# Idle TensorE products, an earlier read of the slot maxima, and a later place for one pair's logits in the last softmax of an attention and slot-MoE kernel

## The chip, the cores and the metric

The kernel runs on one core of a Trainium2 chip. The metric is the device time of one execution in microseconds (us). PE is the matrix engine, DVE the vector engine, ACT the activation engine, POOL the general engine that also issues the loads, SP the engine that issues the stores.

## The reference

The input is q, k and v of 8 batches, 12 heads, 448 tokens and 64 values a head, and the weights phi (768 x 32), w1 (8 experts, 768 x 1024) and w2 (8 experts, 1024 x 768), all float32. The output has 3584 rows of 768.

```python
scores = scale * q @ k^T ;  m = max(scores, -1)
e = exp(scores - m)
attn = e / (sum(e) + exp(-m) + 1e-9)
x = (attn @ v) as rows of 768            # 3584 x 768, heads side by side
logits = x @ phi                         # 3584 x 32 slots
d = softmax of logits over the 3584 rows # for each slot
slot_input = d.T @ x                     # 32 x 768, four slots for each expert
slot_out[e] = relu(slot_input[e] @ w1[e]) @ w2[e]
c = softmax of logits over the 32 slots  # for each row
out = c @ slot_out
```

The softmax `d` runs over all rows, so no expert can start before the last batch's logits are known. This is where the change lies.

## The kernel before

The order of work is written out by hand; each engine carries out its own list in order, and waits are added where one engine reads what another wrote. Two engines that read the same PSUM tile are ordered as well.

Attention goes by pairs of heads: 48 pairs, six to a batch, numbered 0 to 47. The main loop takes a step `s` for each pair, with two halves, numbered `hs = 2*s + y`. In a half step `Bk` makes scores and exponentials, `AV` multiplies the exponentials with v (`AV(n, i, range(3))` for three of four groups of query rows, `AV(n, i, [3])` for the last group), `N1` and `N2` normalize a pair's rows, and `PX` transposes them with four products and copies the result (`xT`) to bf16, on ACT at line 450 (for the last pair half on ACT at line 447 and half on DVE at line 448). In `N2` of the last pair DVE makes the factors and scales three quarters of the rows (lines 407 to 414), and ACT scales the last quarter twice (line 420).

`P(b)` makes the softmaxes of a batch as a list of functions, which the dictionary `post` puts into half steps. The last batch's list is `last`:

- `l_mm([j])` multiplies pair j's transposed rows with phi in both orientations: four products into `ps_lT` (line 486, slots on partitions) and four into `ps_l` (line 477, rows on partitions). Both are parts of one PSUM tile. For pair 0 of the batch the order is reversed.
- `l_ev` copies `ps_l` to SBUF on ACT (line 493). `l_turn` takes the maxima of `ps_lT` on DVE (line 507).
- `s_max` spreads the maxima to all partitions with one product (line 517), reduces them and joins them with the running maximum. `d_sub` subtracts, `exps` takes exponentials on ACT (line 529), `corr` rescales the running sums.
- `s_mm` adds the batch's slot inputs: 28 products (line 544). `s_last` adds them to the running sums and makes the experts' input on DVE (lines 561 to 568).
- `keep_busy(n)` issues n products of 128 x 256 whose result nobody reads (`ps_idle`, line 435).

Pair j of the last batch is pair 42 + j, so "pair 47" is its sixth and last. `last[0]` to `last[3]` (the logits of its first four pairs) are in `post`; `last[3]` falls into half step 96. There it stands between the two parts of pair 47's products with v: `AV(47, 2..3, range(3))`, then `post`, then `AV(47, i, [3])`, `PX(46)`, `N1(47)`, `N2(47)`. Behind the loop POOL gets two weight loads (`load_rows`) and two small operations on `own4`, DVE some small operations on constants (lines 718 to 724), and then follow:

```python
keep_busy(1)
last[4]()
PX(NPAIR - 1)
keep_busy(1)
last[5]()
load_rows(35, 37)
load_rows(37, 40)
```

Then the experts, in two groups of four experts side by side. `hidden` makes the w1 products (line 741: 72 in a row for group 0 and half of group 1, later 24), ACT applies relu (line 743), `turn` transposes (lines 748, 749), and `slots` makes the w2 products (line 755), of 384 columns, four experts abreast. `slots(0, range(4))` comes first (32 products), then a transpose, then 96 in a row: `slots(0, range(4, 8))`, and for each half of the output columns `slots(1, range(8), [half])`, row by row of the weights with the four experts of group 1 inside. The w2 weights of experts 3 to 7 are loaded late, row by row (40 rows of 128 x 768), into SBUF that attention frees: `load_rows(37, 40)` brings expert 7's rows 5 to 7 over the batch's x tile, which `s_mm` reads. All weight loads are issued by POOL (line 112).

The output stage multiplies with `c` (line 811), scales on ACT and DVE (lines 817, 819) and stores from SP (line 822) in seven transfers.

Of the kernel before, what the change touches and what calls it, by code (L numbers as in the profile page):

```python
# [31 lines left out]
def kernel(  # L32
# [10 lines left out]
    nc = tc.nc  # L43
    B, H, S, D = q.shape
    DD = H * D
    NS = moe_phi.shape[1]
# [3 lines left out]
    KC = DD // 128  # L50
    FK = F // 128
    ND = DD // 2
    PB = H // 2
    NPAIR = B * PB
# [18 lines left out]
    phi_sb = const.tile([128, KC, NS], BF16, name="phi_sb")  # L73
# [26 lines left out]
    xT = lambda b, j: part("xTa", j * 512, 512) if b < B - 1 and j < 4 else part("xTb", (j % 2) * 512, 512)  # L100
# [32 lines left out]
    with ExitStack() as at:  # L133
# [296 lines left out]
        def keep_busy(n):  # L430

            if "idle" not in st:
                st["idle"] = pb_("ps_idle")
            for _ in range(n):
                nc.tensor.matmul(st["idle"][:, 0:256], ident, w_sb["w1", 0][:, 0, 0:256], start=True, stop=True)

        def PX(n):
            b, pb = divmod(n, PB)
            x, c = xb[b % 2], slice(pb * 128, pb * 128 + 128)
            two = n == NPAIR - 1  # L440
            pss = [pb_("ps_x") for _ in range(1 + two)]
            for i in range(4):
                o = (i % 2 if two else i) * 128
                nc.tensor.matmul(pss[i // 2 if two else 0][:, o:o + 128], x[:, i, c], ident if i < 3 else ident2,  # L444
                                 start=True, stop=True)
            if two:
                nc.scalar.copy(xT(b, pb)[:, 0:256], pss[0][:, 0:256])
                nc.vector.tensor_copy(xT(b, pb)[:, 256:512], pss[1][:, 0:256])
            else:
                nc.scalar.copy(xT(b, pb), pss[0])  # L450
# [7 lines left out]
        def P(b):  # L458
# [3 lines left out]
            v = {}  # L462
# [3 lines left out]
            def l_mm(js):  # L466
                if js[0] == 0:
                    if b < B - 1:
                        v["ps_l"] = pa([128, 4, NS], F32, "ps_l")
                    else:  # L470
                        t = psV.tile([128, 512], F32, tag="v", name="ps_l")
                        v["ps_l"] = t[:, 0:4 * NS].rearrange("p (i s) -> p i s", i=4)
                        v["ps_lT"] = t[:, 4 * NS:4 * NS + 128]

                def plain(j):
                    for i in range(4):
                        nc.tensor.matmul(v["ps_l"][:, i, :], xT(b, j)[:, i * 128:(i + 1) * 128], phi_sb[:, j, :],
                                         start=(j == 0 and i == 0), stop=(j == KC - 1), skip_group_check=True)

                for j in js:  # L480
                    if b < B - 1 or j == 0:
                        plain(j)
                    if b == B - 1:

                        for i in range(4):
                            nc.tensor.matmul(v["ps_lT"][NS * i:NS * i + NS, :], phi_sb[:, j, :],
                                             xT(b, j)[:, i * 128:(i + 1) * 128],
                                             start=False, stop=(j == KC - 1), skip_group_check=True)
                        if j:
                            plain(j)  # L490

            def l_ev():
# [33 lines left out]
            def exps(z0=0, z1=8):  # L526
                if "cd" not in v:
                    v["cd"] = psm.tile([128, 8, NS], BF16, tag="cd", name="cd", bufs=1)
                nc.scalar.activation(flat(v["cd"][:, z0:z1, :]), flat(v["z"][:, z0:z1, :]), AF.Exp)
# [40 lines left out]
            both = lambda *fs: (lambda: [f() for f in fs])  # L570
            if b < B - 1:
                return [both(lambda: l_mm(range(KC)), l_ev, c_max), both(l_turn, c_sub), both(s_max, d_sub),
                        both(exps, corr)] + ([c_turn, both(s_mm, s_add)] if late(b) else [both(s_mm, s_add), c_turn])
            return [lambda: l_mm([0]), lambda: l_mm([1]), lambda: l_mm([2]), lambda: l_mm([3]), lambda: l_mm([4]),
                    both(lambda: l_mm([PB - 1]), l_ev, l_turn, lambda: keep_busy(1), s_max,
                         d_sub, lambda: exps(4, 8), corr, lambda: keep_busy(4), s_mm, s_last, lambda: keep_busy(2),
                         c_max, c_sub, lambda: exps(0, 4)),
                    c_turn]

# [2 lines left out]
        post = {}  # L582
        for b in range(B - 1):
            for z, f in enumerate(P(b)):
                at_z = (0, 1, 2, 4, 6, 9) if late(b) else (0, 1, 2, 3, 4, 6)
                post.setdefault(2 * (PB * b + PB + 2) + at_z[z], []).append(f)
# [9 lines left out]
        hrec = psm.tile([128, 1], F32, name="hrec", bufs=1)  # L596
        cscale = take(F + (KC + 10) * NS, 8 * B).bitcast(F32).rearrange("p (h b i) -> p h b i", h=2, i=4)
        last = P(B - 1)
        for z in range(4):
            post.setdefault(2 * NPAIR - 5 + 2 * z - (z == 3), []).append(last[z])  # L600


        runs = [(n, i) for n in range(NPAIR) for i in range(4)]
# [118 lines left out]
        nc.gpsimd.affine_select(out=own4, in_=own4, fill=1.0, compare_op=ALU.not_equal, base=0,  # L722
                                pattern=[[-16, 2], [-36, 4], [-1, 4]], channel_multiplier=1)
        nc.vector.reduce_max(own, own4, axis=AX.X)
        keep_busy(1)
        last[4]()
        PX(NPAIR - 1)
        keep_busy(1)
        last[5]()
        load_rows(35, 37)  # L730
        load_rows(37, 40)
# [46 lines left out]
        for half in range(2):  # L778
            for bp in range(B // 2):
                o = (half * (B // 2) + bp) * 4  # L780
                nc.tensor.matmul(ps_cs[:, o:o + 4], cT[:, bp, half, :, :].rearrange("p b j -> p (b j)"), band,
                                 start=True, stop=True)
# [70 lines left out]
```

## Time and profile before

| | us |
|---|---|
| median of 3 runs | 311.84 (311.04 to 312.73) |
| profiled execution, its own time | 313.42 |
| its span, first to last instruction | 311.6 |
| PE busy | 279.1 (90%) |
| DVE busy | 250.9 (81%) |
| ACT busy | 247.4 (79%) |
| POOL busy | 196.9 (63%) |
| mean granted TensorE clock | 0.944 |

The profile is one execution. A timeline row gives the start and length in us from the span's start, engine, line, operation, output and input tile, count, and in brackets the idle time before it with what ended it. A row of the windows gives, for a stretch of time, each engine's busy time and count, then the granted PE clock (1 is full speed), the mean busy share of the 16 DMA engines and GB/s. PE rows end where the model of the pipeline has the last result, which is later than the point at which the next product starts.

### The profile page before, as it was taken

The numbers are of one execution on the slowest core, as the hardware profiler recorded it, in microseconds if no ns is written. First come the engines' busy times: TensorE is split into PE (matmuls) and PEld (weight loads), VectorE is DVE, ScalarE is ACT, GpSimd is POOL, SyncE is SP. The second block draws the span as 40 slices with busy tenths as digits, with TensorE's granted clock in tenths as the row PEclk, the third lists the DMA queues.
The fourth block names the chain that finished last, engine by engine and source line by source line (L and its number), as shares of the span: only waits on it lengthen the run. The fifth ranks groups of instructions, "written<-read, shape, count | busy, mean of one in ns | idle before, by whom it ended". The sixth has DMA issues, their size and how long they took to land.

```text
span 311.6 us, 12145 instructions
## 1 busy us (share of the span) xinstructions
PE 279.1 (90%) x5070; PEld 160.7 (52%) x5070; DVE 250.9 (81%) x575; ACT 247.4 (79%) x546; POOL 196.9 (63%) x402
## 2 busy tenths in 40 slices
PE   2899899999999999999999999999999996997800
PEld 1444466565566566656556665566655554461100
DVE  4777999999989999998999899989997455237910
ACT  2357499999999999999899999998999984218700
POOL 8642778879878987697979688976776713000000
PEclk9999999999999999999999999999999998697555
DMA  6990399999999999687999999999445999935997
GB/s 86 150 130 12 45 203 207 198 190 169 190 196 166 208 172 208 78 129 126 207 156 187 171 203 154 194 181 160 79 53 103 161 191 210 211 72 214 449 439 312
DMA packets 36934, 54.30 MB, mean 174 GB/s; under 512 B 2576, under 2 KB 27664, under 8 KB 36496
## 3 DMA queue, kind: packets, MB, share of 16 engines
q0 software_dynamic: 35872, 42.52, 84.8%
q1 hardware_dynamic: 1008, 11.01, 8.3%
q8 instruction: 39, 0.64, 0.8%
q14 instruction: 15, 0.12, 0.1%
HBM read 85.03 MB, written 11.01 MB: 308 GB/s over the span
## 4 chain that ended last, share of the span: by engine, by line
PE 68%; DVE 15%; ACT 6%; issue 3%; POOL 3%; POOLq 0%
PE ps_av L386 14%; PE ps_a L240 10%; PE ps_t L216 7%; PE ps_b L320 6%; DVE mx L242 6%; PE ps_b L323 6%; PE ps_b L349 5%; DVE mx L253 3%; PE ps_b L352 3%; PE ps_o L811 3%; PE ps_x L444 3%; PE ps_h L741 2%; PE ps_a L249 2%; PE ps_s L544 2%; ACT W L817 2%
## 5 line engine op out<-in xcount | busy, mean ns | idle before, releaser
L242 DVE TENSOR_REDUCE mx<-ps_a 128x1 f32<-128x448 f32 x246 | 135.3, 612 | 3.3 <-PE ps_a L240 2.6
L325 ACT ACTIVATE W<-ps_b 128x448 bf16<-128x448 f32 x246 | 118.4, 575 | 0.2 <-PE ps_a L240 0.2
L240 PE MATMUL ps_a<-W 64*128 64x448 bf16 x246 | 79.9, 352 | 0.0
L320 PE MATMUL ps_b<-W 64*128 64x448 bf16 x246 | 67.8, 352 | 0.3
L323 PE MATMUL ps_b<-mT,sel 64*128 64x448 bf16 x246 | 65.5, 350 | 0.0
L386 PE MATMUL ps_av<-W 128*128 128x65 bf16 (+1 forms) x1536 | 65.2, 196 | 0.3 <-issue 0.3
L386 PEld LDWEIGHTS <-W 128*128 128x128 bf16 (+1 forms) x1536 | 50.4, 101 | 27.6 <-issue 23.6
L414 POOL TENSOR_TENSOR W<-ubuf,rec 128x384 bf16<-128x384 f32 x44 | 36.2, 823 | 37.8 <-DVE rec L408 24.3
L355 ACT ACTIVATE W<-ps_b 128x448 bf16<-128x448 f32 x90 | 47.5, 568 | 8.0 <-PE ps_b L352 8.0
L216 PEld LDWEIGHTS <-W 64*64 64x64 bf16 x1344 | 31.2, 113 | 19.2 <-issue 8.0
L216 PE MATMUL ps_t<-ident,W 64*64 64x64 bf16 x1344 | 32.1, 198 | 5.8 <-DMA W<-in_q_dram 4.2
L112 POOL DMA_DIRECT2D W<-in_moe_w_dram x37 | 24.7, 669 | 13.7 <-PE ps_s L544 5.1
L450 ACT CAST W<-ps_x 128x512 bf16<-128x512 f32 x47 | 28.1, 599 | 5.9 <-PE ps_x L444 5.7
L262 DVE TENSOR_REDUCE mx<-ps_a 128x1 f32<-128x448 f32 x48 | 29.4, 613 | 0.6 <-PE ps_a L259 0.3
L349 PE MATMUL ps_b<-W 64*64 64x448 bf16 (+1 forms) x138 | 28.9, 380 | 0.1
L240 PEld LDWEIGHTS <-W 64*128 64x128 bf16 x246 | 23.0, 94 | 9.8
L219 ACT COPY W<-ps_t 128x896 bf16<-128x896 bf16 x20 | 18.8, 940 | 11.3 <-PE ps_t L216 11.1
L253 DVE TENSOR_REDUCE mx<-ps_a 128x1 f32<-128x448 f32 x42 | 23.7, 617 | 4.5 <-PE ps_a L249 4.2
L352 PE MATMUL ps_b<-mT,sel 64*64 64x448 bf16 (+1 forms) x138 | 27.0, 362 | 0.0
L323 PEld LDWEIGHTS <-sel 64*128 64x128 bf16 x246 | 20.0, 94 | 12.4 <-issue 2.2
L398 ACT COPY ubuf<-ps_av 128x455 f32<-128x455 f32 x44 | 25.2, 574 | 1.2 <-PE ps_av L386 1.0
L423 POOL TENSOR_TENSOR W<-ubuf,rec 128x128 bf16<-128x128 f32 x44 | 17.5, 398 | 3.7
(133 smaller groups left out, 440.1 us busy)
## 6 DMA issues: line engine op xcount, KB each, us to landing
W<-in_moe_w_dram POOLq DMA_DIRECT2D x25, 768.0 KB, 9.8
out_dram<-W SPq DMA_DIRECT2D x3, 2688.0 KB, 11.1
W<-in_v_dram POOLq DMA_DIRECT2D x32, 192.0 KB, 6.2
W<-in_q_dram POOLq DMA_DIRECT2D x15, 336.0 KB, 6.6
W<-in_k_dram POOLq DMA_DIRECT2D x15, 336.0 KB, 7.4
W<-in_moe_w_dram POOLq DMA_DIRECT2D x5, 576.0 KB, 10.1
out_dram<-W SPq DMA_DIRECT2D x3, 768.0 KB, 4.2
W<-in_moe_w_dram POOLq DMA_DIRECT2D x1, 960.0 KB, 9.7
```

What stands on the lines that cost most here:

```text
L216: nc.tensor.transpose(ps[r, a, c:c + 64], src[r, pl, tok * D:(tok + 1) * D], ident[r, r])
L240: nc.tensor.matmul(ps[:, 0:S], t[r, 0, i * 128:(i + 1) * 128], t[r, 1, :], start=True, stop=True)
L242: nc.vector.reduce_max(m[:, c:c + 1], ps[:, 0:S], axis=AX.X)
L253: nc.vector.reduce_max(mx[g][:, c:c + 1], pss[hl][:, 0:S], axis=AX.X)
L320: nc.tensor.matmul(pss[hl][:, 0:S], t[rs[hl], 1, cols], t[rs[hl], 0, :], start=True, stop=False)
L323: nc.tensor.matmul(pss[hl][:, 0:S], sel[rs[hl], 2 * pl + hl:2 * pl + hl + 1].to_broadcast([64, 128]), mT[mg(n)][rs[hl], :], start=False, s ...
L325: nc.scalar.activation(e[:, hl, :], pss[hl][:, 0:S], AF.Exp, scale=scale)
L349: nc.tensor.matmul(outs[hl], t[rs[hl], 1, cols], t[rs[hl], 0, :], start=True, stop=False)
L352: nc.tensor.matmul(outs[hl], sel[rs[hl], 2 * pl + hl:2 * pl + hl + 1].to_broadcast([64, m]), mT[mg(n)][rs[hl], :], start=False, stop=True)
L355: nc.scalar.activation(e, p[:, 0:S], AF.Exp, scale=scale)
L386: nc.tensor.matmul(o, eT[n, i, hl][:, qc], vp[g % 2][:, 2 * pl + hl, i, 0:W65], start=(i == 0 and u == 0 and hl == 0), stop=(i == 3), skip ...
L414: eng.tensor_mul(x[:, 0:3, c:c + 128].rearrange("p i (h d) -> p i h d", h=2), u[:, 0:6, 0:D].rearrange("p (i h) d -> p i h d", h=2), rec[: ...
```

## The change

1. The fourth pair's logits, `last[3]`, leave half step 96 and are called behind the loop, so they stand behind `AV(47, i, [3])` and `PX(46)` on PE.
2. Idle products: ahead of `last[4]` six in place of one, ahead of `last[5]` two in place of one, behind the last logits two in place of one, behind the spread of the maxima twelve in place of four.
3. `l_turn` comes ahead of `l_ev`: DVE reads the maxima from PSUM first, ACT copies the logits afterwards.
4. The last pair's logits go by halves: two products into `ps_lT` and two into `ps_l` for the first two row tiles, then the same for the other two.

No instruction of DVE, ACT or POOL is added or removed. POOL's and SP's order is the same; on ACT and DVE only the waits of the two readers differ. PE gets 15 more idle products.

```diff
-                def plain(j):
-                    for i in range(4):
+                def plain(j, tiles=range(4)):
+                    for i in tiles:
                         nc.tensor.matmul(v["ps_l"][:, i, :], xT(b, j)[:, i * 128:(i + 1) * 128], phi_sb[:, j, :],
...
-                        for i in range(4):
-                            nc.tensor.matmul(v["ps_lT"][NS * i:NS * i + NS, :], phi_sb[:, j, :],
-                                             xT(b, j)[:, i * 128:(i + 1) * 128],
-                                             start=False, stop=(j == KC - 1), skip_group_check=True)
-                        if j:
+                        for i0 in (0, 2):
+                            for i in (i0, i0 + 1):
+                                nc.tensor.matmul(v["ps_lT"][NS * i:NS * i + NS, :], phi_sb[:, j, :],
+                                                 xT(b, j)[:, i * 128:(i + 1) * 128],
+                                                 start=False, stop=(j == KC - 1), skip_group_check=True)
+                            if j == KC - 1:
+                                plain(j, (i0, i0 + 1))
+                        if 0 < j < KC - 1:
                             plain(j)
...
-                    both(lambda: l_mm([PB - 1]), l_ev, l_turn, lambda: keep_busy(1), s_max,
-                         d_sub, lambda: exps(4, 8), corr, lambda: keep_busy(4), s_mm, s_last, lambda: keep_busy(2),
+                    both(lambda: l_mm([PB - 1]), l_turn, l_ev, lambda: keep_busy(2), s_max,
+                         d_sub, lambda: exps(4, 8), corr, lambda: keep_busy(12), s_mm, s_last, lambda: keep_busy(2),
                          c_max, c_sub, lambda: exps(0, 4)),
...
-        for z in range(4):
-            post.setdefault(2 * NPAIR - 5 + 2 * z - (z == 3), []).append(last[z])
+        for z in range(3):
+            post.setdefault(2 * NPAIR - 5 + 2 * z, []).append(last[z])
...
-        keep_busy(1)
+        last[3]()
+        keep_busy(6)
         last[4]()
         PX(NPAIR - 1)
-        keep_busy(1)
+        keep_busy(2)
         last[5]()
```

## The prediction

> **What bounds the kernel now.** I read the 40 slices of the page first: PE is busy nearly everywhere, so only a stretch where it is not can pay. The clock row falls in two places, near 263 and at the end. I then asked for busy time by windows, and set the windows after finding the clock's steps.
>
> ```profile
> core 0: us, PE busy (x) PEld busy (x) DVE busy (x) ACT busy (x) POOL busy (x), PEclk, DMA share, GB/s
> 263.00:264.00 1.00, 0.80 (x5) 0.61 (x6) 0.58 (x3) 0.00 (x0) 0.56 (x1) 0.61 1.09 212
> 270.00:271.00 1.00, 1.00 (x24) 0.53 (x20) 0.00 (x0) 0.06 (x1) 0.00 (x0) 0.98 1.02 201
> 283.00:284.00 1.00, 0.64 (x4) 0.19 (x4) 1.00 (x2) 1.00 (x3) 0.00 (x0) 0.85 0.00 0
> ...
> 256.39:259.81 3.42, 3.11 (x63) 2.24 (x61) 1.96 (x8) 2.04 (x5) 0.53 (x1) 1.00 1.04 209
> 259.81:263.22 3.41, 1.82 (x24) 1.06 (x24) 2.15 (x8) 1.72 (x5) 1.62 (x5) 1.00 1.13 212
> 263.22:266.63 3.41, 2.93 (x43) 1.73 (x47) 2.02 (x8) 0.43 (x2) 0.93 (x2) 0.50 1.03 212
> 266.63:270.05 3.42, 3.42 (x40) 1.28 (x36) 0.89 (x5) 1.00 (x2) 0.00 (x0) 0.50 1.00 205
> 270.05:273.46 3.41, 3.41 (x65) 1.76 (x61) 0.66 (x2) 1.37 (x2) 0.00 (x0) 1.00 1.09 218
> 280.29:283.70 3.41, 1.53 (x18) 0.60 (x15) 1.81 (x3) 2.25 (x4) 0.00 (x0) 1.00 0.00 0
> ```
>
> A mean clock of 0.61 in the first row puts the step from 1 to 0.5 at 263.22; 0.98 puts the return at 270.04, 0.85 the next drop at 283.70. The steps are 6.82 and 13.66 us apart, two and four times 3.41. On that grid the clock falls after a window in which PE was busy for 1.82 of 3.41 us (53%) and after one with 1.53 (45%); 3.11 (91%) kept it, and 2.93 (86%, at half clock) did not bring it back. So the last softmax's chain costs twice: by its own length, and by 6.8 us of half clock.
>
> Next the timeline, which carries the chain.
>
> ```profile
> 257.92 0.53 PE L386 MATMUL ps_av<-W 128*128 128x65 bf16 x12
> 258.12 0.58 ACT L450 CAST W<-ps_x 128x512 bf16<-128x512 f32 x1
> 258.75 0.24 PE L486 MATMUL ps_l<-W,phi_sb 128*32 128x128 bf16 x4 [0.31 <-ACT W L450]
> 259.12 0.32 PE L386 MATMUL ps_av<-W 128*64 128x65 bf16 x8
> 259.38 0.40 PE L444 MATMUL ps_x<-ident,W 128*128 128x128 bf16 x4
> 259.49 0.17 DVE L407 SCALAR_TENSOR_TENSOR rec<-ps_av,ec 128x7 f32<-128x7 f32 x1 [1.29 <-PE ps_av L386]
> 259.61 0.27 PE L435 MATMUL ps_idle<-W,ident 128*128 128x256 bf16 x1
> 259.87 0.58 ACT L450 CAST W<-ps_x 128x512 bf16<-128x512 f32 x1 [1.16 <-PE ps_x L444]
> 259.95 1.06 POOL L112 DMA_DIRECT2D W<-in_moe_w_dram  x2 [2.30 <-PE ps_x L444]
> 260.50 0.24 PE L486 MATMUL ps_l<-W,phi_sb 128*32 128x128 bf16 x4 [0.62 <-ACT W L450]
> 260.65 0.52 ACT L420 ACTIVATE W<-ps_av,rec 128x64 bf16<-128x64 f32 x2 [0.20 <-DVE W L414]
> 260.79 0.67 PE L444 MATMUL ps_x<-ident,W 128*128 128x128 bf16 x4
> 261.52 0.19 DVE L724 TENSOR_REDUCE ubuf<-ubuf 128x2 f32<-128x32 bf16 x1 [0.29 <-POOL ubuf L722]
> 261.62 0.41 DVE L448 CAST W<-ps_x 128x256 bf16<-128x256 f32 x1
> 262.09 0.23 PE L486 MATMUL ps_l<-W,phi_sb 128*32 128x128 bf16 x2 [0.28 <-DVE W L448]
> 262.25 0.27 PE L477 MATMUL ps_l<-phi_sb,W 128*128 128x32 bf16 x4
> 262.56 0.27 ACT L493 COPY lb<-ps_l 128x128 f32<-128x128 f32 x1 [1.03 <-PE ps_l L477]
> 262.85 0.29 DVE L507 TENSOR_REDUCE sm<-ps_l 128x1 bf16<-128x128 f32 x1 [0.82 <-ACT lb L493]
> 263.20 0.29 PE L517 MATMUL ps_bc<-ident,sm 128*128 128x128 bf16 x1 [0.57 <-DVE sm L507]
> 264.80 0.80 PE L544 MATMUL ps_s<-cd,W 128*128 128x32 bf16 x24 [0.46 <-ACT cd L529]
> 266.16 5.97 PE L741 MATMUL ps_h<-W,ubuf 128*32 128x512 bf16 x72
> 276.28 4.08 PE L755 MATMUL ps_so<-W 128*32 128x384 bf16 x96
> ...
> 283.54 13.79 SPq L822 DMA_DIRECT2D out_dram<-W  x7
> ```
>
> The reader is to see a string of one-engine hand-overs from 259.12 to 266.16 with PE mostly waiting, then PE alone to 280.4, then the output, whose queue stays full:
>
> ```profile
> 285.00:310.50 25.50, 9.52 (x41) 1.63 (x40) 11.21 (x12) 9.41 (x11) 0.00 (x0) 0.50 0.99 420
> ```
>
> With a DMA share of 0.99 behind the first output transfer, the end moves one for one with that transfer's start.
>
> **The change part by part.** *Fourth pair's logits behind pair 47's products.* The eight products of 258.75 stood, with a wait of 0.31 us, ahead of the last eight products of pair 47 (259.12), which release its normalization (259.49). Now those eight follow the twelve of 257.92 directly. A row's modelled end lies some 0.16 us behind the next product's start (the pair transposes end at 259.78, the next product starts at 259.61), so they start near 258.45 - 0.16 = 258.29: a gain of 0.83 us; from the full modelled end it would be 0.67. DVE is free by then and everything behind moves by 0.83: normalization 258.66, pair 46's transposes 258.55, their copy on ACT 259.04 to 259.62 (ACT ended the earlier copy at 258.70), the two scalings on ACT to 260.34. POOL's two weight issues (259.95) wait for the same products and move as much; they matter, because L724 on DVE waits for POOL's work behind them and stands ahead of the copy L448. If they didn't move, this gain would be lost: 0 is the lower bound, 0.83 my value, since the last products that read the rows they overwrite are among the moved ones. The moved logits start behind pair 46's transposes at 258.78 and take 0.29 to 0.37 (260.50 to 260.79, 258.75 to 259.12): to 259.07 to 259.15.
>
> *Six idle products.* Nine idle products are in the trace:
>
> ```profile
> L435 PE MATMUL ps_idle<-W,ident x9: 269/417/421, 259.6 to 265.7; 128*128 128x256 bf16 x9
> 263.29 1.06 PE L435 MATMUL ps_idle<-W,ident 128*128 128x256 bf16 x4
> ```
>
> Four at half clock took 1.06, one 0.42: (1.06 - 0.42) / 3 = 0.213 apart, so 0.107 at full clock. Six take 0.64, to 259.71 to 259.79, while the fifth pair's logits wait for ACT until 259.67: at most 0.12 late. That is hidden: their next step, the last pair's transposes, needs its fourth tile from ACT at 260.34 and PE reaches it at 260.2. At half clock the six would take 1.28 and cost 0.4.
>
> *Two idle products before and two after the last pair's logits* (one each before) end inside the waits for ACT and DVE copies: nothing, with about 0.1 us of cover each.
>
> *Logits by halves.* The second half waits for L448 (now 260.79 to 261.20), then has two plain products behind it, not four: the four take 0.27 against some 0.18 for one, so 0.03 each, a gain of 0.05.
>
> *Maxima ahead of the copy.* L507 waited for ACT's copy (262.56 to 262.83). Both read one PSUM tile and the program orders them; now the reduce waits for PE and the copy for the reduce. Gain 262.85 - 262.56 = 0.29. The copy's reader, the subtraction, stands behind the broadcast product and two more steps of DVE, so the copy is covered.
>
> Sum so far 0.83 + 0.05 + 0.29 = 1.17: the broadcast product comes at 262.03, ahead of the step, and takes about 0.07 less at full clock: 1.24.
>
> *Twelve idle products for four* lie between it and the slot sums. At full clock 12 x 0.107 = 1.28 from about 262.1 to 263.4; the slot sums wait for ACT until 264.80 - 1.24 = 263.56. Covered by 0.15. At half clock they take 2.56 and end 1.1 us late.
>
> *The clock.* On this execution's grid the window 259.81 to 263.22 now has gaps only from about 261.1 to 261.26 and 261.9 to 262.03, so PE is busy some 3.1 us of 3.41, the 91% that kept the clock. Then the first expert products, from 264.92, run at full clock. Before, they spent 266.16 to 270.05 at half: 3.89 / 2 = 1.94 us saved. Sum 1.24 + 1.94 = 3.18.
>
> The Trainium skill ("TensorE: Matmul & The Clock Gate", Part 1: The HAM clock gate) has a free-running window of 3413 ns, which agrees with the steps above. Its section "HAM oscillation — how this bites in real kernels" words the rule as no idle gap over about 3.4 us. The trace disagrees: the clock fell with no gap above 0.7 us, so by that rule the added products would buy nothing and the sum would be 1.24.
>
> *What is late next.* The second group's slot products need the last weight rows (expert 7, rows 5 to 7 of 8).
>
> ```profile
> 265.88 0.54 POOL L112 DMA_DIRECT2D W<-in_moe_w_dram  x1 [2.26 <-PE ps_s L544]
> ...
> W<-in_moe_w_dram POOLq DMA_DIRECT2D x1, 576.0 KB, 11.1
> ...
> 273.46:276.87 3.41, 3.41 (x80) 2.25 (x76) 0.82 (x4) 0.69 (x1) 0.00 (x0) 1.00 0.55 110
> 276.87:280.29 3.42, 3.42 (x88) 2.07 (x80) 1.04 (x4) 0.00 (x0) 0.00 (x0) 1.00 0.02 5
> ```
>
> Issued at 265.88, they land 11.1 us later: 276.98. At the queue's 205 to 218 KB a us, 576 KB need 2.8 us; the other 8 are queueing behind earlier rows, and the DMA share is 1.00 or more from 256.39 to 273.46. An issue 1.2 us earlier only waits longer: the landing stays. The first product that reads them is the 24th of the second group (row 5 of 8, fourth expert of four); 32 products of the first group stand ahead, so it is number 56 of the 96 of 276.28: (4.08 - 0.33) / 95 = 0.0395 apart, so 278.45. Slack 1.47 us. Of the 3.18, at most that passes, less some 0.1 for the hand-over: 1.35 us. PE then waits 1.8 us at that product.
>
> **The rivals.** (a) *No wall*: the rows land earlier, because they are issued earlier or the stream isn't full in other executions. All of 3.18: 308.7. For it: the run's own times vary by 1.7 us; against it: shares of 1.00 to 1.13 in each window.
>
> (b) *The wait drops the clock* (the slower side). With 3.18 gained PE would stop at about 275.25 until 277.0. The window 273.46 to 276.87 then has 1.8 us of work in 3.41 (53%), the very share after which the clock fell. Then the last 41 slot products run at half clock: 41 x 0.0395 = 1.6 us, and the selection and first output products 0.3 to 0.7 more: -1.35 + 1.6 + 0.3 = +0.55, to +0.95: 312.4 to 312.8. Against it: those slot products run four abreast, so PE is denser than in the chain's window; and the wait must lie almost wholly in one window, which about half of all positions allow. It decides if 53% of dense work drops the clock.
>
> (c) *The clock still falls at 263.22.* The chain is 1.24 shorter, but 264.92 to 270.05 is half speed, so half of that is given back: 0.62, 311.2. If the step comes earlier, the twelve products are slow too and 1.1 us late: near 311.8.
>
> **How the numbers follow.** The profiled execution took 313.42 (span 311.6 and 1.8 around it), 1.58 above the median 311.84. My sum makes it 312.05. Runs whose window lies otherwise lose less to the clock before, and so gain a little less; I carry 1.35 over to the median as it is: 310.5. Chances: forecast 0.50 (310.5, own range 309.9 to 311.1), (a) 0.17, (b) 0.18, (c) 0.15. For 8 in 10 the range takes in (c) and the lower price of (b), and half way to (a): 309.3 to 312.5. Within 0.5% (1.56 us, about what a measurement of this kernel can tell from no change) is 310.28 to 313.40. Faster than that: all of (a), 0.4 of the forecast, a little of (c): 0.39. Slower: the worst of (b), and a chain delayed by late idle products with the clock low throughout: 0.11. Same: 0.50.
>
> **What would show it.** Right: the reduce of the maxima ends by about 262.0 ahead of the logits' copy; clock 1.00 through 263 to 275; the 72 expert products in about 4.0 us; a PE wait of over 1 us inside the slot products ended by a DMA near 277. Wrong: last rows landing well before 277, no wait there (then a); 0.50 behind the wait (b); slot sums starting behind the twelve idle products, not behind ACT (c).

## The result and the profile after

The changed kernel took 310.73 us (median of 20 runs, 309.53 to 312.25), the kernel before 312.52 (20 runs, 310.86 to 313.83). The ratio is 0.9948, 95% interval 0.9932 to 0.9964: 0.5% faster. By the ratio that is 1.6 us, by the medians 1.8, where 1.35 were forecast. The profiled execution took 310.18, with a span of 308.4.

The timeline of the changed kernel, in the stretch shown before. Line numbers are up to four higher than before from line 486 on. The first row is pair 46's copy on DVE (its last one of line 398). It lies ahead of everything that was changed, and I count from it below. In the trace of before it is at 256.07.

```profile
256.07 0.63 DVE L398 COPY ubuf<-ps_av 128x455 f32<-128x455 f32 x1
```

```profile
255.20 0.63 DVE L398 COPY ubuf<-ps_av 128x455 f32<-128x455 f32 x1
...
257.04 0.78 PE L386 MATMUL ps_av<-W 128*128 128x65 bf16 x20
257.87 0.17 DVE L407 SCALAR_TENSOR_TENSOR rec<-ps_av,ec 128x7 f32<-128x7 f32 x1 [0.55 <-PE ps_av L386]
258.24 0.59 ACT L450 CAST W<-ps_x 128x512 bf16<-128x512 f32 x1 [0.41 <-PE ps_x L444]
258.32 1.06 POOL L112 DMA_DIRECT2D W<-in_moe_w_dram  x2 [1.55 <-PE ps_x L444]
258.36 0.81 PE L435 MATMUL ps_idle<-W,ident 128*128 128x256 bf16 x6
259.11 0.24 PE L487 MATMUL ps_l<-W,phi_sb 128*32 128x128 bf16 x4
260.00 0.41 DVE L448 CAST W<-ps_x 128x256 bf16<-128x256 f32 x1
260.91 0.29 DVE L510 TENSOR_REDUCE sm<-ps_l 128x1 bf16<-128x128 f32 x1 [0.49 <-PE ps_l L477]
261.24 0.27 ACT L496 COPY lb<-ps_l 128x128 f32<-128x128 f32 x1 [1.11 <-DVE sm L510]
261.26 0.23 PE L520 MATMUL ps_bc<-ident,sm 128*128 128x128 bf16 x1 [0.16 <-DVE sm L510]
261.33 1.47 PE L435 MATMUL ps_idle<-W,ident 128*128 128x256 bf16 x12
262.87 0.75 PE L547 MATMUL ps_s<-cd,W 128*128 128x32 bf16 x24
264.17 4.07 PE L745 MATMUL ps_h<-W,ubuf 128*32 128x512 bf16 x72 [0.22 <-DVE ubuf L564]
272.39 2.46 PE L759 MATMUL ps_so<-W 128*32 128x384 bf16 x55
275.20 1.95 PE L759 MATMUL ps_so<-W 128*32 128x384 bf16 x41 [0.35 <-DMA W<-in_moe_w_dram]
...
280.31 13.60 SPq L826 DMA_DIRECT2D out_dram<-W  x7
```

The twenty products of pair 47 with v now stand together. The maxima come ahead of ACT's copy. The 72 expert products take 4.07 us, not 5.97. And the 96 slot products are split after the 55th by a wait for a DMA: the 56th reads the last weight rows, the place named in the prediction. The last load's rows of the issues and the windows on this trace's clock grid:

```profile
263.90 0.54 POOL L112 DMA_DIRECT2D W<-in_moe_w_dram  x1 [1.93 <-PE ps_s L547]
...
W<-in_moe_w_dram POOLq DMA_DIRECT2D x1, 576.0 KB, 11.3
...
258.21:261.62 3.41, 3.11 (x42) 2.04 (x39) 2.23 (x9) 1.74 (x5) 1.68 (x5) 1.00 1.03 203
261.62:265.03 3.41, 3.13 (x57) 2.14 (x59) 2.24 (x11) 0.43 (x2) 0.89 (x2) 1.00 1.10 223
275.27:278.69 3.42, 2.56 (x47) 1.39 (x50) 1.11 (x2) 0.96 (x2) 0.00 (x0) 1.00 0.00 0
```

PE is busy for 3.11 and 3.13 us of 3.41 in the softmax's windows and the clock stays at 1.00. The mean granted clock says the same of the other runs: it is 0.955 to 0.958 in the 20 runs of the changed kernel, and 0.943 to 0.953 in the 49 runs of the kernel before that were made beside the experiments. The last rows land at 263.90 + 11.3 = 275.2, when PE goes on. Without the wait the 56th product would start at 272.39 + 55 x 0.0395 = 274.56: the wait is 0.64 us.

Each step counted from pair 46's copy (a row's start less the start of that copy), for all traces:

```
                       broadcast  slot  first   56th slot  wait  last rows  first output  span's
                       product    sums  expert  product          landed     transfer      end
before                   7.13     8.73  10.08    22.4      0      20.9       27.47        55.58
before, again (e9)       7.21     8.81  10.17    21.8      0      21.1       26.88        55.01
changed                  6.06     7.67   8.97    20.00     0.64   20.0       25.11        53.21
idle only (e1)           7.13     8.68   9.97    20.99     0.6    21.0       26.10        54.21
order only (e2)          6.04     7.65   8.94    21.0      0      20.0       26.08        54.19
no late rows (e3)        6.06     7.67   8.97    19.3      0      20.1       24.45        52.57
late rows last (e4)      6.06     7.67   8.97     -        0      20.0       24.46        52.56
late rows last (e12)     6.06     7.67   8.97     -        0      20.2       24.50        52.62
copy first (e5)          6.36     7.90   9.20    20.14     0.5    20.1       25.25        53.36
logits back (e6)         6.78     8.39   9.69    21.37     1.3    21.3       26.48        54.60
loads, no effect (e7)    6.06     7.67   8.97    20.30     0.9    20.3       25.41        53.53
24 idle (e8)             6.06     8.75  10.05    20.4      0      20.3       25.52        55.29
4 idle of 12 (e10)       6.07     7.67   8.97    20.19     0.8    20.1       25.29        53.41
loads delayed (e11)      6.07     7.68   8.97    21.02     1.6    21.0       26.12        54.25
```

The copy itself stands between 254.37 and 257.39 in these traces, where no kernel differs. That spread is as wide as the scatter of the times, which is why a median of 8 to 12 runs says less here than one trace read from a fixed row. Each line is one execution, though: the steps of the chain agree to 0.1 us between kernels that do not differ in them, the landing to 0.3. e5 to e11 ran only once each, for the trace, and took 310.52, 311.77, 310.16, 313.22, 313.84, 309.61 and 313.48 us, in this order; with that scatter these times are not compared.

### The profile page after: what moved, and what is told of

It reads as the page before. It is cut to its first block, busy times and chain, and to the rows that moved or that the text cites. A ratio compares the mean times of both kernels' runs of the same rounds, so it can differ in the third digit from the quotient of the medians.

```text
span 308.4 us, 12176 instructions
## 1 busy us (share of the span) xinstructions
PE 277.2 (90%) x5085; PEld 160.8 (52%) x5085; DVE 250.7 (81%) x575; ACT 247.1 (80%) x546; POOL 197.4 (64%) x402
## 4 chain that ended last, share of the span: by engine, by line
PE 64%; DVE 15%; ACT 6%; DMA 4%; issue 3%; POOL 3%; POOLq 0%; ACTq 0%
PE ps_av L386 14%; PE ps_a L240 10%; PE ps_t L216 7%; DVE mx L242 6%; PE ps_b L320 6%; PE ps_b L323 6%; PE ps_b L349 5%; DMA W<-in_moe_w_dram 4%; DVE mx L253 3%; PE ps_b L352 3%; PE ps_x L444 3%; PE ps_o L815 2%; PE ps_a L249 2%; ACT W L821 2%; PE ps_s L547 2%
## 6 DMA issues: line engine op xcount, KB each, us to landing
out_dram<-W SPq DMA_DIRECT2D x3, 2688.0 KB, 11.3
```

## The experiments

My theory after the result: the order shortens the chain, the idle products hold the clock, and the last weight rows cut off the rest. The first rival was that the rows are no limit and the wait was chance; the second, that the order alone does it.

**e1: idle products alone.**

```diff
 (kernel before)
-keep_busy(1); last[4]()  ...  keep_busy(1); last[5]()
+keep_busy(6); last[4]()  ...  keep_busy(2); last[5]()
-l_ev, l_turn, keep_busy(1), s_max, ..., keep_busy(4), s_mm
+l_ev, l_turn, keep_busy(2), s_max, ..., keep_busy(12), s_mm
```

> The kernel before with only the idle products changed (6, 2, 2 and 12 for 1, 1, 1 and 4); the order of logits, maxima and copy is the old one. Theory (clock and rows: the idle products hold the clock, and the last weight rows cap what that brings): granted clock 1.00 from 262 to 276, the 72 expert products in 4.1 us and not 6.0, the first of them at most 0.1 us earlier, a DMA wait of 0.1 to 0.6 us inside the slot products, and 1.3 to 1.8 us less time. Rival (the order is what counts; the clock's gain is lost elsewhere): 0 to 0.4 us less. Rival (PE is not kept busy enough without the shorter chain): the clock still falls near 263 and the time is within 0.3 us of before.

Measured: 311.58 (12 runs), ratio to before 0.9973 (0.9948 to 0.9997). In the trace:

```profile
259.74 1.06 POOL L112 DMA_DIRECT2D W<-in_moe_w_dram  x2 [2.29 <-PE ps_x L444]
265.84 4.07 PE L741 MATMUL ps_h<-W,ubuf 128*32 128x512 bf16 x72 [0.22 <-DVE ubuf L561]
276.86 1.95 PE L755 MATMUL ps_so<-W 128*32 128x384 bf16 x41 [0.33 <-DMA W<-in_moe_w_dram]
...
263.00:264.00 1.00, 1.00 (x10) 0.91 (x11) 0.66 (x3) 0.00 (x0) 0.41 (x1) 1.00 0.67 137
```

The clock holds without the shorter chain: the first expert product comes only 0.11 us earlier than before (9.97 for 10.08), but the 72 take 4.07 us. In the trace the end is 1.37 us earlier than in the first trace of before (54.21 for 55.58) and 0.80 earlier than in the second, cut by a wait of 0.6 us. The median gained 0.8 to 1.0, less than the 1.3 expected. The rival by which the clock still falls is out: the mean clock of all 12 runs is 0.954 to 0.959. The rival by which the order is what counts, with 0 to 0.4 us less, is out by the traces; the interval of the medians, 0.1 to 1.6 us, does not exclude it. The two loads of 259.74 stand at 3.87 behind pair 46's copy, as before (3.88), and the row of 263 to 264 shows the stream of weights at 137 GB/s where 205 is usual. This is the first hint at what my prediction missed, though not a clear one: in the first trace of before, with its loads at the same place, the row of 263 to 264 shows 212.

**e2: the order alone.**

```diff
 (changed kernel)
-keep_busy(6), (2), (2), (12)
+keep_busy(1), (1), (1), (4)
```

> The changed kernel with the old counts of idle products (1, 1, 1 and 4): the new order of logits, maxima and copy alone. Theory (clock and rows): the slot sums start 1.0 us earlier behind pair 47's products with v than before, the clock still falls to 0.50 for about 6.8 us around 262 to 270, half of the 1.0 us is given back in expert products at half clock, no wait for a DMA in the slot products, 0.3 to 0.7 us less time. Rival (the order is what counts): 1.2 us less or more.

Measured: 311.77 (12 runs), ratio 0.9983 (0.9960 to 1.0005).

```profile
261.85:265.26 3.41, 2.01 (x39) 1.33 (x38) 1.87 (x7) 0.69 (x3) 0.80 (x2) 1.00 1.11 220
265.26:268.67 3.41, 3.38 (x32) 1.28 (x36) 1.33 (x7) 0.89 (x2) 0.30 (x1) 0.50 1.03 212
...
265.29 5.71 PE L745 MATMUL ps_h<-W,ubuf 128*32 128x512 bf16 x72 [0.22 <-DVE ubuf L564]
```

The chain is 1.1 us shorter (slot sums 7.65), but a window with PE busy 2.01 of 3.41 (59%) drops the clock, for one window and not two, and the 72 take 5.71. End 54.19, 1.4 earlier than in the first trace of before and 0.8 than in the second; the median gained 0.5 to 0.8, with an interval from 0.2 more to 1.25 less, so the medians alone show no gain. In two of the 12 runs the mean clock was 0.957, as in the changed kernel, and in the other ten 0.944 to 0.949: the order alone holds the clock now and then. By the traces each half alone gives some 0.8 to 1.4, the two together 1.8 to 2.4 (53.21 against 55.01 and 55.58). Neither half carries the change.

**e3: the last rows not read.** Rows 0 to 2 stand in for rows 5 to 7 of expert 7. The kernel leaves those rows out, so its output differs from the reference; only its time is of use.

```diff
-w_sb["w2", 4 * g + i][:, kt, ...]
+w_sb["w2", 4 * g + i][:, kt - 5 if 4 * g + i == 7 and kt > 4 else kt, ...]
```

> The changed kernel, except that the second group's products of expert 7 with weight rows 5 to 7 read rows 0 to 2, which landed earlier; the last load is still issued and lands unread, so the output differs from the reference. Theory (clock and rows): no idle time inside the last 96 slot products, which take 4.1 us; the first output transfer comes 0.6 to 1.8 us earlier behind the chain than in the changed kernel, and the time is 2.2 to 2.9 us less than before, against 1.6 to 1.8 for the changed kernel. Rival (the rows were no limit, the 0.35 us of idle in the trace was a chance of that execution): same as the changed kernel, 1.6 to 1.8 less than before.

**e4 and e12: the last rows read last.**

```diff
-for half in range(2):
-    slots(1, range(FK), [half])
+for half in range(2):
+    slots(1, range(5), [half])
+for half in range(2):
+    slots(1, range(5, FK), [half])
     copies[half](so[:, half * ND:(half + 1) * ND], pss[half][:, 0:ND])
```

> The changed kernel with the second group's slot products in another order: both column halves of weight rows 0 to 4 first, then both halves of rows 5 to 7; all products are there. The first product that reads the last load comes 20 products, 0.8 us, later. Theory (clock and rows): the wait for the DMA shrinks by up to 0.8 us and is gone in about half of the executions; the copies of the two halves stand 0.5 us apart and no longer 1.3, which costs 0.1 to 0.2 us at the end; together 0.2 to 0.8 us less than the changed kernel, 1.9 to 2.5 less than before. Rival (the rows are no limit): 0.1 to 0.3 us slower than the changed kernel, 1.4 to 1.6 less than before.

> The reordered slot products of e4 again, for a better mean. Theory (clock and rows): no wait for a DMA in the slot products, end 52.5 to 52.7 counted from pair 46's copy on DVE, time 2.0 to 2.6 us less than before. Rival (the gain in the trace does not reach the median): 1.4 to 1.8 less, as the changed kernel.

Measured: e3 310.84 (8 runs), ratio 0.9948 (0.9923 to 0.9974); e4 310.56, 0.9951 (0.9921 to 0.9981); e12, the same kernel as e4, 309.79, 0.9930 (0.9904 to 0.9955); e4 and e12 with 12 runs each. Of the traces, e3's row and then e12's:

```profile
274.58 4.08 PE L759 MATMUL ps_so<-W 128*32 128x384 bf16 x96
```

```profile
273.58 4.13 PE L759 MATMUL ps_so<-W 128*32 128x384 bf16 x96
277.26 0.56 DVE L795 CAST W<-ps_so 128x384 bf16<-128x384 f32 x1 [2.58 <-PE ps_so L759]
277.75 0.48 ACT L795 CAST W<-ps_so 128x384 bf16<-128x384 f32 x1 [5.48 <-PE ps_so L759]
```

In all three traces the 96 products are one piece again, and the end comes at 52.56 to 52.62, 0.6 us ahead of the changed kernel: just its wait. So the rows are a limit, worth 0.64 us in that execution. The second copy follows the first by 0.5 us and nothing is lost by it. By the medians alone e3 and e4 would have spoken for the rival (0.9948 and 0.9951 against 0.9948); their intervals of 0.5% and 0.6% cannot tell 0.6 us. e12 has the lowest median of the kernels that ran more than once. The traces are clear, the medians lean the same way, and the reordered kernel beats the kernel before in both sets of runs; that it beats the changed kernel is shown by the traces, not by the medians.

**e5: the copy first again.**

```diff
-l_turn, l_ev, keep_busy(2), s_max
+l_ev, l_turn, keep_busy(2), s_max
```

> The changed kernel with ACT's copy of the logits ahead of DVE's maxima again. Times count from the start of pair 46's copy on DVE (line 398, the last one), which lies ahead of everything that is changed; to the end of the span it is 55.58 before and 53.21 changed. Theory (the step is worth 0.27 us on the chain, the last weight rows hide it): broadcast product at 6.33 and not 6.06, slot sums at 7.94 and not 7.67, the DMA wait in the slot products 0.4 us and not 0.68, end 53.2 to 53.3. Rival (the chain sets the end): end 53.5.

```profile
274.51 1.95 PE L759 MATMUL ps_so<-W 128*32 128x384 bf16 x41 [0.25 <-DMA W<-in_moe_w_dram]
```

The broadcast product comes 0.30 us later (6.36), the slot sums 0.23, the end 0.15 (53.36). The wait took up some of the step, with rows that landed 0.1 later. The difference of 0.07 between 0.30 and 0.23 is a price of the change: with the copy behind the maxima, the subtraction on DVE has to wait for ACT as well as for the step before it. The copy is long done by then (at 261.51 in the changed kernel, the subtraction starts at 262.15); what it costs is a second wait, and the subtraction starts 0.11 us behind the step before it, in e5 0.03.

**e6 and e11: the two loads later, with and without the chain.** In e6 the fourth pair's logits go back ahead of pair 47's last products. In e11 only POOL's two loads are held, by a copy that waits for DVE. (e7 was to do this by putting them behind two small operations on POOL. These ran earlier, in POOL's idle time, and the loads kept their place at 3.13; it shows only that the landing varies by 0.3, 20.0 to 20.3, where the issues are the same.)

```diff
 (e6)
-for z in range(3): ...          last[3]() behind the loop
+for z in range(4): post.setdefault(2 * NPAIR - 5 + 2 * z - (z == 3), []).append(last[z])
 (e7, e11)
-load_rows(rows, 35)             ahead of own4's operations
+gpsimd.tensor_copy(<free>, spread[:, 0, :])        # e11 alone
+load_rows(rows, 35)             behind them
```

> The changed kernel with the fourth pair's logits back ahead of pair 47's last products with v. Counted from pair 46's copy on DVE. The chain and POOL's two loads behind pair 47's products come 0.75 us later. Theory (those two loads are issued so late that the stream of rows has a gap, so their issue sets when the last rows land): last rows land at 20.9 and not 20.0, the wait in the slot products grows to 0.8 to 0.9, end 54.1 to 54.2. Rival (the full stream alone sets the landing, as in my prediction): landing stays at 20.0, no wait or 0.1, end 53.3 to 53.4.

> The changed kernel with POOL's two loads behind pair 47's products issued after POOL's two small operations on own4, some 1.2 us later; nothing else moves. Counted from pair 46's copy on DVE. Theory (their issue opens a gap in the stream of rows): the last rows land at 21.2 and not 20.0, PE's chain is as before it (slot sums at 7.7), the wait in the slot products is 1.8 to 2.0 us, end 54.4. Rival (the full stream alone sets the landing): landing 20.0, wait 0.65, end 53.2. If the long wait also drops the clock (rival b of the prediction), 0.50 behind it and an end of 55.5 or more.

> The changed kernel with POOL's two loads behind pair 47's products held back by a POOL copy that reads a tile that DVE writes late (the copy's result is overwritten later): their issue at 4.7 and 5.2 and not 3.13 and 3.65, counted from pair 46's copy on DVE; PE's chain as in the changed kernel. Theory (their issue opens a gap in the stream of rows): the last rows land at 21.3 or later and not 20.0 to 20.3, the wait in the slot products is 1.9 us or more, end 54.5 or later. Rival (the full stream alone sets the landing, as in my prediction): landing 20.0 to 20.3, wait 0.7 to 1.0, end 53.2 to 53.5. If the long wait drops the clock (rival b of the prediction), 0.50 behind it and 1.6 us more.

First e6, then e11:

```profile
258.83 1.06 POOL L112 DMA_DIRECT2D W<-in_moe_w_dram  x2 [2.29 <-PE ps_x L444]
264.38 0.54 POOL L112 DMA_DIRECT2D W<-in_moe_w_dram  x1 [1.93 <-PE ps_s L547]
276.33 1.95 PE L758 MATMUL ps_so<-W 128*32 128x384 bf16 x41 [0.99 <-DMA W<-in_moe_w_dram]
...
262.00:263.00 1.00, 1.00 (x11) 0.90 (x10) 0.81 (x3) 0.01 (x1) 0.46 (x1) 1.00 0.85 166
...
W<-in_moe_w_dram POOLq DMA_DIRECT2D x1, 576.0 KB, 11.9
```

```profile
262.07 1.12 POOL L112 DMA_DIRECT2D W<-in_moe_w_dram  x2 [0.31 <-PE ps_x L444]
265.86 0.53 POOL L112 DMA_DIRECT2D W<-in_moe_w_dram  x1 [1.96 <-PE ps_s L547]
278.17 1.95 PE L760 MATMUL ps_so<-W 128*32 128x384 bf16 x41 [1.34 <-DMA W<-in_moe_w_dram]
...
276.88:280.30 3.42, 2.13 (x42) 1.29 (x42) 0.56 (x1) 0.15 (x1) 0.00 (x0) 1.00 0.08 17
...
W<-in_moe_w_dram POOLq DMA_DIRECT2D x1, 576.0 KB, 12.3
```

With the loads at 3.87 (e6) the rows land at 21.3, with the loads at 4.92 (e11) at 21.0, against 20.0 to 20.3 with the loads at 3.13 in nine traces. In e11 the chain is untouched up to the slot products, and the wait grows from 0.64 to 1.63 us and the end from 53.21 to 54.25. In e11 the last load itself is issued at 8.70, as in the changed kernel, so it is the two loads that move the landing. The sizes are not the theory's. In e11 I expected 1.9 us of wait and an end of 54.5; in e6 I expected the rows at 20.9 and the end at 54.2, and got 21.3 and 54.60. And e11 issues the two loads 1.05 us later than e6, yet its rows do not land later. So the two issues move the landing by about 1 us, but not one for one. e6 also prices the moved logits: 1.4 us at the end, 0.72 of chain and the rest through the landing. The waits of 1.3 and 1.6 us did not drop the clock: rival (b) did not happen in the longest wait tried, which left PE 2.13 us of work in its window.

**e8 and e10: 24 and 4 idle products for twelve.**

```diff
-keep_busy(12), s_mm
+keep_busy(24), s_mm             (e8)
+keep_busy(4), s_mm              (e10)
```

> The changed kernel with 24 idle products in place of 12 behind the broadcast product. Counted from pair 46's copy on DVE. At full clock 24 x 0.107 = 2.57 us, so the slot sums start at 8.7 and not 7.67, behind the idle products and not behind ACT. Theory (the last rows hide part of it): landing 20.0 to 20.2, no wait in the slot products, end 53.5 to 53.8. Rival (the last load's own issue, which also comes 1.0 us later, sets its landing): landing 21.0, wait 0.65, end 54.2.

> The changed kernel with four idle products in place of twelve behind the broadcast product (the other counts are the new ones). PE's busy share in the worst window falls from some 0.89 by 8 x 0.107 = 0.86 us to some 0.64; traced so far: 0.53 and less dropped the clock, 0.83 and more kept it. Theory (the threshold lies under 0.6, so the twelve are more than is needed): clock 1.00 throughout, the end 53.2 counted from pair 46's copy on DVE. Rival (all twelve are needed): the clock falls to 0.50 near the slot sums, the 72 expert products take 5 us or more, end 53.8 to 54.5.

First e8, then e10:

```profile
264.81 0.75 PE L547 MATMUL ps_s<-cd,W 128*128 128x32 bf16 x24
265.84 0.54 POOL L112 DMA_DIRECT2D W<-in_moe_w_dram  x1 [3.01 <-PE ps_s L547]
274.33 4.08 PE L759 MATMUL ps_so<-W 128*32 128x384 bf16 x96
...
281.58 14.01 SPq L826 DMA_DIRECT2D out_dram<-W  x7
```

```profile
261.06:264.48 3.42, 2.26 (x51) 1.34 (x53) 2.27 (x10) 0.43 (x2) 0.68 (x2) 1.00 1.07 218
```

Twenty-four delay the slot sums by 1.08 us (8.75), as priced. The first output transfer is only 0.41 later (25.52 for 25.11): the wait for the rows takes up the rest. The last load is issued 1.08 us later as well, at 9.78, as late as in the kernel before (9.81), and yet it lands at 20.3, with the two loads ahead of it at 3.13. So the rival here, that its own issue sets its landing, is out. That the span ends at 55.29 is another thing: it closes 29.8 us behind the first output transfer, all other kernels 28.1, since in this execution one of the 16 parts in which the last store lands came some 1.7 us after the others. Four keep the clock in this trace and the end at 53.41, so the twelve are more than that execution needed; one place of the window does not show that four suffice at every place. The window has PE busy for 66%. My expectation, that 53% and less had dropped the clock so far, left out e2, where 59% dropped it.

**e9: the kernel before, again.**

> The kernel before, unchanged, once more, for a second place of the clock's window. Counted from pair 46's copy on DVE (first trace: slot sums 8.73, first expert product 10.08, end 55.58). Theory (the chain is fixed, the half clock's place is not): slot sums within 0.1 of 8.73, the clock falls at another point between 4 and 9, the 72 expert products take between 4.5 and 6.5 us, end between 54.2 and 56.0. Rival (what differs between executions lies in this stretch's chain itself): slot sums off by more than 0.2.

```profile
259.51:262.92 3.41, 2.32 (x36) 1.50 (x36) 2.05 (x8) 1.62 (x5) 1.46 (x4) 1.00 1.01 200
...
267.21 5.30 PE L741 MATMUL ps_h<-W,ubuf 128*32 128x512 bf16 x72
```

Slot sums 8.81, end 55.01, the 72 expert products 5.30 us for 5.97: the chain is the same and the clock's place costs 0.6 us more or less.

## Why the prediction was right, and where not

*The moved logits*: 0.83 forecast, 0.75 measured (pair 47's normalization 3.42 to 2.67); the last eight of the twenty products start at 2.30, not at the 2.22 that I had from the modelled end of the twelve less 0.16, and then take the same 0.37 to the normalization as before.

*Six idle products* end 0.2 us too late for the fifth pair's logits (259.11, ACT's copy done at 258.83), not 0.12, and it is hidden as forecast: L448 keeps the gain of 0.75 (260.00 - 255.20 = 4.80, before 261.62 - 256.07 = 5.55).

*Halves and maxima*: 0.34 forecast; the broadcast product gained 1.07, less 0.75 makes 0.32. e5 prices the copy alone at 0.30.

*Twelve idle products* are covered: e10 with four has the same start of the slot sums, 7.67. *The slot sums* gained 1.06, not 1.24: 0.08 from the first step, the rest mostly the second wait of the subtraction (0.07, e5). The copy itself is covered, as I had said; the wait instruction was a term that I had not counted.

*The clock* held, and the 72 products fell by 1.90 us; 1.94 were forecast. The chain up to the slot products gained 17.98 - 14.97 = 3.01; forecast 3.18.

*What is late next* is the step that failed in size. The wait is at the product that I named, and it ends with the last rows, but I held their landing fixed and it moved by 0.95 us (20.91 to 19.96). Of the last load's own issue the sentence "An issue 1.2 us earlier only waits longer: the landing stays" is right: e8 issues it 1.08 us later and the rows land at 20.3. What it misses are POOL's two issues ahead of it. I had counted them as moved with the chain and then left them out of the landing. With the two at 3.13 the last rows land at 20.0 to 20.3 in nine traces, with the two at 3.87 or later at 20.9 to 21.3 in five, among them e11, which moves nothing else.

How the two issues do it is shown only in part. I had read a DMA share of 1.00 to 1.13 as a full stream. From 6 to 8 us behind pair 46's copy the rows come at 225 to 237 GB/s in the nine traces and at 187 to 199 in e1, e6, e9 and e11; at 205 KB a us this gap is worth 0.3 to 0.5 us. But the first trace of before has 222 there. The rest of the move lies at the very end: the last load lands in 16 parts, and the last of them comes 1.6 to 2.3 us behind the first in the five traces, 1.2 to 1.5 in the nine. Why the parts drift apart stays open.

So the wait took 0.64 of the gain, not 1.8, and 2.36 passed to the first output transfer (27.47 to 25.11). (Slack less hand-over, 1.47 - 0.1, is 1.37 and not 1.35, which changes nothing; the hand-over took 0.04.) The median gained only 1.6 to 1.8. That other executions of before lose less to the clock, as e9 does with its end at 55.01, would explain it, but two traces do not prove it.

That 310.73 came so near to 310.5 is in part luck. The base of three runs, 311.84, lay 0.68 below the median of 20, and the gain was forecast 0.44 too small: two errors that cancel in part. Of the signs that I had named, the maxima ahead of the copy, the clock of 1.00 and the 4.07 us of the expert products came; the wait of over 1 us did not.

Rival (a), no wall, came half true: the rows landed earlier, since two loads were issued earlier, but a wall of 0.64 us stayed, which e3, e4 and e12 give back. Rival (b) did not come; it needed a window with 1.8 us of work, and the longest wait left 2.13 (e11), so its own number was not tried. Rival (c), the clock still falling, did not come in any of the eleven traces with the new idle counts or near them. The Trainium skill ("TensorE: Matmul & The Clock Gate", HAM oscillation — how this bites in real kernels) words its rule as no idle gap of PE above some 3.4 us. By it the idle products would have brought nothing. The measurement decides against it: in e1 they took 1.9 us off the 72 expert products of the first trace of before, 1.2 off those of the second, and the clock fell after windows of this chain without an idle gap of even 1 us (0.62 the longest in both traces of before, 0.94 in e2).

## What to carry to other kernels

When a chain is shortened, follow the transfers whose issue it carries, all of them and not only the one that is waited for, and look at the bytes a us as well as at the busy share: here a share of 1.1 to 1.2 over 2 us stood beside 187 to 199 GB/s in some traces and 225 to 237 in others. Idle products are worth adding where a sparse stretch stands ahead of dense matrix work, as many as end before the wait that they fill, and the product that reads the last transfer is best put last. Where executions scatter, compare traces from a fixed row ahead of the change.

## What the runs showed of the hardware that was not expected

The busy share of a window does not tell whether the clock falls: 2.32 of 3.41 us dropped it (e9), 2.26 (e10) and 2.13 (e11) kept it. The windows that kept it hold dense or wide products. An idle product of 256 columns takes 0.107 us, which is 2.4 columns a ns. Each product's columns at this rate, times the part of the 128 x 128 array that its weights fill, come to 0.20, 0.29 and 0.31 of the window in those that dropped the clock (before, e9, e2), and to 0.37, 0.47 and 0.48 in three that kept it (e2 one window earlier, e1, e10). This is a reading of few windows, not tried by itself.

One load lands in 16 parts over 1.2 to 2.4 us, and the reader waits for the slowest (the last part comes at 19.96, the 56th product starts at 20.00). And the traces whose clock records begin with a step at 18.0 to 19.0 us reach pair 46's copy at 254.4 to 256.1, those with a step at 22.7 to 24.5 at 255.2 to 257.4; I did not try whether the one causes the other.
